# Attention and a routed expert layer on one core: first reads of scattered rows through a view of their own, weight pieces sent in another order

## The chip, the cores and the metric

One Trainium2 chip, one of its eight cores. The metric is the time of one execution on the device, in microseconds (us); each figure for the kernel is the median of several executions. The engines are PE (TensorE), with its weight loads shown as PEld, DVE (VectorE), ACT (ScalarE), POOL (GpSimd) and SP (SyncE, which here only issues DMAs). POOL issues DMAs too, the indirect ones among them. POOLq and SPq are the sequencers of these engines.

## The reference

Linear attention with a decay per head, over q, k and v of shape (4, 8, 768, 64), is computed in blocks of 64; its output, seen as 3072 tokens of 512 values, goes into a layer of 8 experts, each token to the one expert whose embedding has the largest cosine with it:

```python
for b in range(nb):
    intra = np.einsum('bhic,bhjc->bhij', qb, kb) * Dmask[None]
    out[:, :, sl] = np.einsum('bhij,bhjd->bhid', intra, vb) + np.einsum('bhid,bhde->bhie', qb * lam_pow[None], kv_state)
    kv_state = lam_block * kv_state + np.einsum('bhsd,bhse->bhde', kb * rev_pow[None], vb)
...
logits = xn @ en.T / tau                      # x and the embeddings scaled to norm 1
expert_idx = np.argmax(logits, axis=1)        # gate_w: the softmax there
out[mask] = gate_w[mask, None] * (np.maximum(x[mask] @ w1[e], 0.0) @ w2[e])
```

w1 is (8, 512, 1024), w2 (8, 1024, 512).

## The kernel before, in words

**Attention.** The 3072 tokens are 24 tiles of 128. A Python loop over rounds i = -2 to 23 writes the program out; round i finishes tile i of attention (transposes of q and k, scores, output, state) and prepares the next ones. Each engine works its own instructions strictly in the order in which they are written; semaphores between the engines are put in by the framework from what each instruction reads and writes. SP only issues loads: q, k and v into a ring of three buffers each, some rounds ahead, and staging loads. POOL scales k (`pool_ks`) and issues everything listed below.

**Routing.** The tiles are grouped (four groups of 4, four of 2). When a group's last tile is done, PE computes its logits, DVE the one-hot choice; `rt_n` (L530) takes the square root of the squared norms on POOL; PE and DVE find each token's rank within its expert (`pe_rank`, `rt_b`), DVE scales the logits by the norm (`rt_c`, L573 to L576), ACT takes the exp (L579), and DVE the gate (`rt_d`). In what follows a root is one `rt_n`. The root of the group of tiles 20 and 21 is written in round 22, the last (tiles 22 and 23) after the loop. ACT's exps stand in program order among its evictions of the first expert layer (L845).

**Scatter and read.** `scatter` (L588) writes the 128 rows of a tile by an indirect DMA into `xs_dram`, a buffer in DRAM in which each expert has its own range; a row carries the token's values in fp16, its number and its gate. Every tile scatters through its own view (`xs_views`), which the framework takes to be disjoint from the other tiles'. Reads are indirect DMAs of 128 rows (`gather`, L644) out of the whole of `xs_dram`: a read waits for all scatters written before it, and a scatter waits for all reads written before it. Experts 0 to 3 are read in two steps. `load_a` reads their first 256 rows (two reads of 128) in rounds 20 and 22, as far as the tokens of tiles 0 to 17 reach (`count("A")`); three small operations on POOL (L652, L654, L656) make the row indices ahead of each read, and rows beyond the count are skipped. `load_x` and `load_q4` read the remainder later, with indices from all tiles, and wait for the last scatter.

**Weights.** The 32 weight pieces (two per expert and matrix) come in two ways. 17 are loaded by POOL with a cast to fp16 on the way (`load_w`, L325; 8 into a weight pool, 9 into buffers of the q, k and v ring once these are done with), in a fixed order of the experts; the rounds are in the list `WP`. 15 are staged in fp32 by SP (`stage`, L338; three buffers, the first three loads in the rounds of `WS`) and cast by DVE in the tail (`cast`, `more_w`).

**Order on POOL.** A small planner (`at`, `run`) puts steps into slots of a round: `pooln` comes before `pool_ks`, `pool0` and `pool` at the round's end. In round 20 stand the reads of experts 0 and 1, in 21 the scatters of tiles 18 and 19 and three pieces, in 22 the root of tiles 20 and 21, the reads of experts 2 and 3 and three pieces, in 23 the scatters of tiles 20 and 21 and two pieces.

**The tail.** A first-step block A (256 tokens) for experts 0 to 3, then the remainders B of these, then experts 4 to 7 whole (E): transposes, first layer `pe_L1` (L842, evicted by ACT with relu, three PSUM banks), second layer `pe_L2` (L880), scaling on DVE (L860), and a scattered result on POOL (`put`, L861; five result buffers). The last 32 rows of two times four experts share blocks of their own (Q). PE starts expert 0's first layer ahead of the last group's routing. `asks` says after which block's result POOL is to issue which remaining read; a table in the function's tail writes it out.

## Time and profile before

| | us |
|---|---|
| median of 3 runs (lowest, highest) | 264.95 (262.96, 266.25) |
| the profiled execution, whole | 266.45 |
| its span, first to last instruction | 264.6 |

All rows come from the profiled execution. Times in them are us from the start of its span, if not marked ns. In a timeline a row is a run of like instructions: its start, its length, engine, line, operation, what it writes and reads, the count, and in brackets how long the engine was idle before it and what ended that. "issue" is time for which the profile shows no wait. For DMAs, the length on POOL is the time to issue them, not that of the transfer.

### The profile page before, as it was taken

The numbers are of one execution on the slowest core, as the hardware profiler recorded it, in microseconds if no ns is written. First come the engines' busy times: TensorE is split into PE (matmuls) and PEld (weight loads), VectorE is DVE, ScalarE is ACT, GpSimd is POOL, SyncE is SP. The second block draws the span as 40 slices with busy tenths as digits, with TensorE's granted clock in tenths as the row PEclk, the third lists the DMA queues.
The fourth block names the chain that finished last, engine by engine and source line by source line (L and its number), as shares of the span: only waits on it lengthen the run. The fifth ranks groups of instructions, "written<-read, shape, count | busy, mean of one in ns | idle before, by whom it ended". The sixth has DMA issues, their size and how long they took to land. (4 is left out here: it accounts for less than half of the span.)

```text
span 264.6 us, 7554 instructions
## 1 busy us (share of the span) xinstructions
PE 224.0 (85%) x3118; PEld 170.7 (65%) x3118; DVE 134.9 (51%) x367; ACT 118.6 (45%) x257; POOL 140.9 (53%) x215
## 2 busy tenths in 40 slices
PE   0889999999999999979959429987289999999990
PEld 0678888999889888857845415765067665555640
DVE  1385668579497486846604039212055539272131
ACT  5355646664755643625406022433045573644600
POOL 3375451676354648654576674278744646532332
PEclk9999999999999999999997957999869999999997
DMA  6999999999999999989339599988429996941312
GB/s 154 237 255 208 213 215 229 210 213 251 217 232 219 187 256 224 201 206 418 115 74 207 141 202 221 389 260 211 160 54 350 412 355 222 394 173 40 121 50 76
DMA packets 71684, 56.68 MB, mean 214 GB/s; under 512 B 52179, under 2 KB 64471, under 8 KB 69728
## 3 DMA queue, kind: packets, MB, share of 16 engines
q1 hardware_dynamic: 64576, 34.62, 48.6%
q0 software_dynamic: 6928, 21.55, 32.5%
q8 instruction: 25, 0.41, 0.7%
q14 instruction: 11, 0.09, 0.1%
q10 hardware_dynamic: 144, 0.00, 0.0%
HBM read 55.88 MB, written 9.99 MB: 249 GB/s over the span
## 5 line engine op out<-in xcount | busy, mean ns | idle before, releaser
L845 ACT ACTIVATE hT<-h_ps 128x416 f16<-128x416 f32 (+3 forms) x60 | 32.0, 540 | 44.3 <-PE h_ps L842 26.9
L372 POOL TENSOR_TENSOR ks<-kn,kdec 128x512 f32<-128x512 f32 x24 | 25.2, 1049 | 37.8 <-PE kaz L456 15.2
L861 POOL DMA_INDIRECT out_dram<-y_sb,tags x24 | 25.6, 1066 | 31.5 <-DVE y_sb L860 15.2
L860 DVE TENSOR_SCALAR y_sb<-y_ps,tags 128x512 f32<-128x512 f32 x24 | 18.0, 751 | 38.3 <-PE y_ps L880 28.1
L418 DVE TENSOR_TENSOR stm<-s_ps,step 128x512 f32<-128x512 f32 x48 | 30.8, 684 | 12.6 <-PE s_ps L410 12.6
L880 PEld LDWEIGHTS <-hT 128*128 128x128 f16 x192 | 18.3, 101 | 29.1 <-ACT hT L845 8.9
L842 PEld LDWEIGHTS <-w_sb 128*128 128x128 f16 x208 | 22.2, 119 | 21.5 <-issue 15.5
L880 PE MATMUL y_ps<-w_sb,hT 128*128 128x512 f16 x120 | 30.5, 404 | 6.4 <-ACT hT L845 6.1
L842 PE MATMUL h_ps<-xTe,w_sb 128*128 128x416 f16 (+2 forms) x176 | 26.2, 305 | 10.2 <-ACT hT L845 8.6
L410 PE MATMUL s_ps<-qT,kT 64*64 64x128 f32 x768 | 29.4, 284 | 1.2 <-issue 1.1
L588 POOL DMA_INDIRECT xs_dram<-xg,si x24 | 24.7, 1028 | 10.2 <-issue 4.0
L439 PE MATMUL ob<-stm,vn 128*64 128x128 f32 x384 | 26.6, 279 | 0.5 <-issue 0.5
L410 PEld LDWEIGHTS s_ps<-qT,kT 64*64 64x64 f32 x768 | 22.5, 137 | 5.7 <-issue 3.9
L439 PEld LDWEIGHTS ob<-stm,vn 128*64 128x64 f32 x384 | 20.5, 136 | 4.9 <-issue 4.7
L448 ACT COPY xT<-ob 128x256 f32<-128x256 f32 x24 | 9.0, 374 | 28.3 <-PE ob L439 27.4
L386 DVE TENSOR_TENSOR qT<-q_ps,lamq 128x512 f32<-128x512 f32 x24 | 16.4, 685 | 9.5 <-PE q_ps L384 8.1
L396 PE MATMUL k_ps<-ident,ks 128*128 128x128 f32 x96 | 15.8, 292 | 6.3 <-POOL ks L372 6.3
L644 POOL DMA_INDIRECT x<-xs_dram,rows x16 | 17.3, 1081 | 4.5 <-POOL x L662 3.0
L384 PE MATMUL q_ps<-ident,qr 128*128 128x128 f32 x96 | 17.1, 304 | 1.8 <-DVE qT L386 1.6
L398 ACT COPY kT<-k_ps 128x512 f32<-128x512 f32 x24 | 14.0, 584 | 5.5 <-PE k_ps L396 5.5
L396 PEld LDWEIGHTS k_ps<-ident,ks 128*128 128x128 f32 x96 | 12.3, 151 | 6.3 <-POOL ks L372 6.3
L481 PE MATMUL xps<-ident,xT 128*128 128x128 f32 x96 | 15.5, 277 | 1.0 <-DVE xT L449 1.0
(172 smaller groups left out, 393.8 us busy)
## 6 DMA issues: line engine op xcount, KB each, us to landing
w_st<-in_moe_w_dram SPq DMA_DIRECT2D x15, 1024.0 KB
kn<-in_k_dram SPq DMA_DIRECT2D x24, 256.0 KB
qn<-in_q_dram SPq DMA_DIRECT2D x12, 512.0 KB
vn<-in_v_dram SPq DMA_DIRECT2D x24, 256.0 KB
w_sb<-in_moe_w_dram POOLq DMA_DIRECT2D x8, 512.0 KB
kn<-in_moe_w_dram POOLq DMA_DIRECT2D x3, 512.0 KB
qn<-in_moe_w_dram POOLq DMA_DIRECT2D x3, 512.0 KB
vn<-in_moe_w_dram POOLq DMA_DIRECT2D x3, 512.0 KB
```

The costliest lines, as they stand in the source:

```text
L372: nc.gpsimd.tensor_tensor(ks[i], kn[i], kdec[:, i % RB].unsqueeze(2).to_broadcast([P, H, D]), op=ALU.mult)
L396: nc.tensor.transpose(t[:, hp, :], ks[i][:, 2 * hp : 2 * hp + 2, :].rearrange("p h d -> p (h d)"), ident)
L410: nc.tensor.matmul(bank["s", h2][ds(64 * c, 64), hp, :], kT[i][ds(64 * h2, 64), hp, ds(64 * c, 64)], q_of(i, hp)[ds(64 * h2, 64)], start=( ...
L418: nc.vector.tensor_tensor(stm[i][:, h2], bank.pop(("s", h2)), step.unsqueeze(1).to_broadcast([P, HP, P]), op=ALU.mult)
L439: nc.tensor.matmul(OB[h2][ds(64 * u, 64), b2, :], vn[i][:, 2 * hp + h2, :], stm[i][:, h2, hp, :], start=(i % RB == 0 and b2 == 0), stop=Tr ...
L588: nc.gpsimd.indirect_dma_start(out=xs_views[groups[gi][j]], out_offset=bass.IndirectOffsetOnAxis(ap=slot_i[gi][:, j : j + 1], axis=0), in_ ...
L644: nc.gpsimd.indirect_dma_start(out=out, out_offset=None, in_=xs_dram[:], in_offset=bass.IndirectOffsetOnAxis(ap=idx, axis=0), bounds_check ...
L842: nc.tensor.matmul(h_ps[:, ds(n * (fc - f0), n)], w1_cols(w, c, fc), xTe[k][:, c, 0:n], start=(fc == f0 and c == 0), stop=(c == DC - 1), s ...
L845: nc.scalar.activation(hT[k][:, f0:f1, 0:n], h_ps[:, 0 : n * (f1 - f0)].rearrange("p (f t) -> p f t", t=n), AF.Relu)
L860: nc.vector.tensor_scalar(y, y_ps, tag[:, 1:2].bitcast(FP32), None, op0=ALU.mult)
L861: nc.gpsimd.indirect_dma_start(out=out_views[n_scat[0]], out_offset=bass.IndirectOffsetOnAxis(ap=tag[:, 0:1], axis=0), in_=y[:], in_offset ...
L880: nc.tensor.matmul(y_ps, hT[k][:, fc, ds(P * (g - g_first(k)), P)], w2_rows(w, fc), start=(fc == 0), stop=(fc == FC - 1))
```

## The change

The first reads go through a view of their own, index R of one view more, so that the framework sees no overlap between them and any scatter; in its place each of these reads is made to depend by hand on the scatters of tiles 0 to 17 (`NE = 18`), recorded as they are written. `load_a` becomes one set of three index operations per expert (128x2 instead of 128x1), and `read_a` a read. POOL's order from round 20 on is written out as a list in which pieces, reads and scatters alternate: 13 pieces stand in the loop instead of 16, six of them up to round 16 and one round earlier in four cases, none in rounds 17 to 19; one follows the last root, and three instead of one stand after the last group's scatters. The three first staging loads move to round 23 of SP's order. In the tail the remaining reads are requested after other blocks.

```diff
...
     QN = P // QW
     NQ = E // QN
     GL = len(groups) - 1
-
-    WP = [3, 6, 9, 12, 14, 16, 17, 18, 21, 21, 21, 22, 22, 22, 23, 23]
-    WS = [19, 20, 20]
+    NE = 18
+    WP = [2, 5, 8, 11, 14, 16]
+    WS = [23, 23, 23]
     group_of = {}
     for gi, tl in enumerate(groups):
         for j, t in enumerate(tl):
...
     moe_t = ctx.enter_context(tc.tile_pool(name="moe_t", bufs=1))
     xs_dram = dram.tile([E * ROWS, DM2], I32, name="xs_dram")
-    xs_views = dram_disjoint_views(xs_dram[:], R)
+    xs_views = dram_disjoint_views(xs_dram[:], R + 1)
     n_out = E * GE + NQ
     out_views = dram_disjoint_views(out, n_out)
...
         nc.vector.tensor_reduce(es, rt[gi]["pe"], axis=AXL.X, op=ALU.add)
         nc.vector.reciprocal(xg[gi][:, 0:nt, DW + 1 : DW + 2].bitcast(FP32), es.unsqueeze(2))
+    written = []
     def scatter(gi, j):
-        nc.gpsimd.indirect_dma_start(
+        got = nc.gpsimd.indirect_dma_start(
             out=xs_views[groups[gi][j]],
             out_offset=bass.IndirectOffsetOnAxis(ap=slot_i[gi][:, j : j + 1], axis=0),
             in_=xg[gi][:, j, :],
             in_offset=None,
         )
+        if groups[gi][j] < NE:
+            written.append(got.ins.name)
     xe, xTe, hT = {}, {}, {}
     tags = const.tile([P, E, GE, 2], I32, name="tags")
...
                                 cnt_e.unsqueeze(2).to_broadcast([P, E, GE]), op=ALU.is_ge)
         nc.vector.scalar_tensor_tensor(rows, bad, float(OOB_IDX), row3, op0=ALU.mult, op1=ALU.add)
-    def gather(out, idx):
-        nc.gpsimd.indirect_dma_start(
-            out=out, out_offset=None, in_=xs_dram[:],
+    def gather(out, idx, src):
+        return nc.gpsimd.indirect_dma_start(
+            out=out, out_offset=None, in_=src,
             in_offset=bass.IndirectOffsetOnAxis(ap=idx, axis=0),
             bounds_check=E * ROWS - 1, oob_is_err=False)
+    after = mybir.DependencyInfo(mybir.DependencyClass.Sync, mybir.DependencyReason.DATA)
     def load_a(e):
         xe[e] = X3[e]
-        for g in range(GA):
-            nc.gpsimd.tensor_scalar(bad[:, e, g : g + 1], pos3[:, g : g + 1], cnt_a[:, e : e + 1],
-                                    float(OOB_IDX), op0=ALU.is_ge, op1=ALU.mult)
-            nc.gpsimd.tensor_tensor(bad[:, e, g : g + 1], bad[:, e, g : g + 1], row3[:, e, g : g + 1],
-                                    op=ALU.add)
-            nc.gpsimd.tensor_copy(rows_a[:, e, g : g + 1], bad[:, e, g : g + 1])
-            gather(xe[e][:, g, :], rows_a[:, e, g : g + 1])
+        nc.gpsimd.tensor_scalar(bad[:, e, 0:GA], pos3[:, 0:GA], cnt_a[:, e : e + 1],
+                                float(OOB_IDX), op0=ALU.is_ge, op1=ALU.mult)
+        nc.gpsimd.tensor_tensor(bad[:, e, 0:GA], bad[:, e, 0:GA], row3[:, e, 0:GA], op=ALU.add)
+        nc.gpsimd.tensor_copy(rows_a[:, e, :], bad[:, e, 0:GA])
+    def read_a(e, g):
+        got = gather(xe[e][:, g, :], rows_a[:, e, g : g + 1], xs_views[R])
+        for name in written:
+            tc.add_manual_dep(got.ins, name, after, reason="rows scattered so far")
     def load_x(e, g0, g1):
         if e >= ES:
             xe[e] = X3[e % ES]
             nc.gpsimd.memset(xe[e][:, g0:g1, DW : DW + 1], OOB_IDX)
         for g in range(g0, g1):
-            gather(xe[e][:, g, :], rows[:, e, g : g + 1])
+            gather(xe[e][:, g, :], rows[:, e, g : g + 1], xs_dram[:])
     def load_q4(t):
-        gather(XQ[t][:, 0, :], rowsh[:, t : t + 1])
+        gather(XQ[t][:, 0, :], rowsh[:, t : t + 1], xs_dram[:])
     def width(k):
         return {"A": CA, "B": CE - CA, "E": CE}[k[0]]
...
             at(n + 2, "z", rt_d, gi)
         else:
             at(n + 1, "end", rt_d, gi)
-    for gi, when in enumerate([(6, 7, 8, 9), (10, 11, 12, 13), (14, 15, 16, 17), (17, 18, 18, 19), (19, 19),
-                               (21, 21), (23, 23)]):
+    for gi, when in enumerate([(6, 7, 8, 9), (10, 11, 12, 13), (14, 15, 16, 17), (17, 18, 18, 19), (19, 19)]):
         for j, i in enumerate(when):
-            first = j + 1 < len(when) and when[j + 1] == i and i < 20 and gi < 4
+            first = j + 1 < len(when) and when[j + 1] == i and i < 19
             at(i, "pooln" if first else "pool", scatter, gi, j)
     for n in range(ES):
         at(1 + 2 * n, "pool", clear, X3[n])
     at(20, "pe", count, "A")
-    for i, e in ((20, 0), (20, 1), (22, 2), (22, 3)):
-        at(i, "pool0", load_a, e)
     for i in WP:
         at(i, "pool", load_w)
+    for i, fn, *a in ((20, load_a, 0), (20, read_a, 0, 0), (20, read_a, 0, 1), (20, load_w),
+                      (20, load_a, 1), (20, read_a, 1, 0), (20, load_w), (20, read_a, 1, 1),
+                      (21, scatter, 5, 0), (21, load_w), (21, scatter, 5, 1),
+                      (22, load_a, 2), (22, read_a, 2, 0), (22, load_w), (22, read_a, 2, 1), (22, load_w),
+                      (23, load_a, 3), (23, read_a, 3, 0), (23, load_w), (23, read_a, 3, 1),
+                      (23, scatter, 6, 0), (23, load_w), (23, scatter, 6, 1)):
+        at(i, "pool", fn, *a)
     for i in WS:
         at(i, "sp2", stage)
...
             nc.vector.tensor_copy(mx, nsum)
         A, B, X = [[(n, e) for e in range(E)] for n in "ABE"]
-        asks = {("A", 0, 0): [(None, 0), (0, 2), (1, 2)], ("A", 0, 1): [(2, 2), (3, 2)],
-                ("A", 1, 0): [(None, 1)]}
-        later_x = [(4, 0), (4, 1), (5, 0), (5, 1), (4, 2), (5, 2), (6, 0), (6, 1), (6, 2), (7, 0), (7, 1), (7, 2)]
-        asked_by = [("A", 2, 0), ("A", 2, 1), ("A", 3, 0), ("A", 3, 1)] + [("B", e, GA) for e in range(ES)]
-        asked_by += [("Q", 0, 0), ("E", 4, 0), ("E", 4, 1), ("E", 4, 2)]
+        asks = {("A", 1, 0): [(None, 0)], ("A", 1, 1): [(0, 2)], ("A", 2, 0): [(1, 2), (None, 1)],
+                ("A", 2, 1): [(2, 2)], ("A", 3, 0): [(3, 2)]}
+        later_x = [(4, 0), (4, 1), (4, 2), (5, 0), (5, 1), (5, 2), (6, 0), (6, 1), (6, 2), (7, 0), (7, 1), (7, 2)]
+        asked_by = [("A", 3, 1), ("A", 3, 1), ("B", 0, GA), ("B", 0, GA)] + [("B", e, GA) for e in range(1, ES)]
+        asked_by += [("Q", 0, 0), ("E", 4, 0), ("E", 4, 1), ("E", 4, 2), ("E", 5, 0)]
         for who, what in zip(asked_by, later_x):
             asks.setdefault(who, []).append(what)
...
         rt_a(GL)
         rt_a2(GL)
         rt_n(GL)
+        load_w()
         for buf in XQ:
             clear(buf)
         pe_L1(A[0], range(2, 8))
...
         pe_L2(A[0], 1)
         count("E")
         rows_of_e()
-        ask("A", 0, 0)
-        ask("A", 0, 1)
+        load_w()
+        load_w()
         load_w()
         more_w()
         more_w()
```

## Rows read from the trace of the kernel before

**Rows 1.** The page's first part: busy time, share of the span, instructions of PE.
```profile
PE 224.0 (85%) x3118; PEld 170.7 (65%) x3118; DVE 134.9 (51%) x367; ACT 118.6 (45%) x257; POOL 140.9 (53%) x215
```

**Rows 2.** The list of waits: who waited for whom, us in all, times, longest.
```profile
DVE nrm L573 <- POOL nrm L530: 16.0, 2, 10.0
...
PE h_ps L842 <- ACT hT L845: 12.4, 2, 8.6
...
ACT hT L845 <- remote: 9.0, 3, 5.1
```

**Rows 3.** PE's timeline in the seam: start, duration, work, idle time before and its releaser.
```profile
133.71 1.94 PE L842 MATMUL h_ps<-xT,w_sb 128*128 128x256 f16 x16
139.44 1.86 PE L842 MATMUL h_ps<-xT,w_sb 128*128 128x256 f16 x8 [3.79 <-ACT hT L845]
...
145.82 2.79 PE L842 MATMUL h_ps<-xTe,w_sb 128*128 128x256 f16 x24
157.24 1.86 PE L842 MATMUL h_ps<-xTe,w_sb 128*128 128x256 f16 x8 [8.62 <-ACT hT L845]
...
182.24 2.37 PE L842 MATMUL h_ps<-xTe,w_sb 128*128 128x160 f16 x32 [1.58 <-issue]
...
190.84 1.46 PE L880 MATMUL y_ps<-w_sb,hT 128*128 128x512 f16 x3 [4.87 <-ACT hT L845]
...
194.39 3.51 PE L842 MATMUL h_ps<-xTe,w_sb 128*128 128x160 f16 x32
...
199.69 2.38 PE L842 MATMUL h_ps<-xTe,kn 128*128 128x160 f16 x32
```

**Rows 4.** POOL's timeline from round 19 to the first full read.
```profile
114.39 0.96 POOL L588 DMA_INDIRECT xs_dram<-xg,si  x1 [0.31 <-issue]
...
116.87 0.19 POOL L656 CAST rows_a<-bad 128x1 int32<-128x1 f32 x1
...
121.58 1.16 POOL L644 DMA_INDIRECT x<-xs_dram,rows_a  x1 [4.52 <-DMA xs_dram<-xg,si]
...
126.86 1.10 POOL L644 DMA_INDIRECT x<-xs_dram,rows_a  x1 [0.54 <-POOL rows_a L656]
...
129.42 1.10 POOL L644 DMA_INDIRECT x<-xs_dram,rows_a  x1 [0.53 <-POOL rows_a L656]
133.23 1.03 POOL L588 DMA_INDIRECT xs_dram<-xg,si  x1 [2.71 <-DMA x<-xs_dram,rows_a]
134.57 0.99 POOL L588 DMA_INDIRECT xs_dram<-xg,si  x1 [0.30 <-issue]
135.55 1.72 POOL L325 DMA_DIRECT2D kn<-in_moe_w_dram  x3
137.26 0.78 POOL L530 TENSOR_TENSOR nrm<-nsq_all,half 128x2 f32<-128x2 f32 x1
...
151.44 1.06 POOL L588 DMA_INDIRECT xs_dram<-xg,si  x1 [1.21 <-DMA x<-xs_dram,rows_a]
...
154.99 0.76 POOL L530 TENSOR_TENSOR nrm<-nsq_all,half 128x2 f32<-128x2 f32 x1
...
170.02 1.09 POOL L644 DMA_INDIRECT xq<-xs_dram,rowsh  x1 [7.65 <-DMA xs_dram<-xg,si]
```

**Rows 5.** SP's timeline: its last v loads and the staging loads.
```profile
102.60 11.23 SPq L147 DMA_DIRECT2D vn<-in_v_dram  x3
113.87 88.33 SPq L338 DMA_DIRECT2D w_st<-in_moe_w_dram  x9
```

**Rows 6.** Stretches: busy time of each engine, granted clock (PEclk), DMA share, GB/s.
```profile
138.00:140.00 2.00, 0.56 (x3) 0.41 (x3) 1.44 (x9) 1.32 (x5) 1.09 (x5) 0.68 1.01 172
146.00:148.00 2.00, 2.00 (x20) 2.00 (x19) 0.00 (x0) 0.00 (x0) 1.27 (x4) 1.00 0.32 105
162.00:164.00 2.00, 2.00 (x10) 0.79 (x9) 2.00 (x4) 0.00 (x0) 0.36 (x1) 0.85 1.07 158
...
180.00:190.00 10.00, 4.08 (x46) 3.01 (x43) 0.75 (x1) 1.47 (x4) 7.95 (x11) 1.00 0.58 186
```

## The prediction

> **What bounds the kernel now.** I read the page first, then the waits, then the timelines of PE and POOL over the seam where attention ends and the expert layers begin. PE is busy for 85% of the span [rows 1], and outside the seam it hardly stops, so what counts is when PE gets through the seam. The list of waits names a chain: ACT's evictions of the first layer make PE wait 12.4 us in two pieces, and DVE's norms wait 16.0 us in two pieces for POOL's roots [rows 2]. The PE timeline shows the two pieces: 3.79 us ahead of 139.44 and 8.62 us ahead of 157.24 [rows 3]. Both have one cause. ACT evicts in program order behind an exp, the exp waits for DVE's scaled logits, these wait for a root on POOL, and the root stands behind everything that the rounds before put on POOL. The roots end at 137.26 + 0.78 = 138.04 and 154.99 + 0.76 = 155.75 [rows 4]; PE goes on 1.4 and 1.49 us later. So in the seam POOL's instruction order is the bound, not its arithmetic. From 194.39 PE runs at full load to the end, so what arrives earlier there ends earlier.
>
> A third stop is of another kind: ACT waits for something that the profile calls "remote", 9.0 us in three pieces [rows 2], and PE stands still for 4.87 us of it ahead of 190.84 [rows 3].
>
> **The chain on POOL, step by step.** From the first read (121.58) to the end of the last root (155.75) POOL takes 34.17 us [rows 4].
>
> Waits of scatters on reads. Scatters 18 and 20 waited 2.71 and 1.21 us for reads to land, because reads and scatters went through one view. With a view of its own for the reads, a scatter needs only the 0.30 us that the second scatter takes to be issued (133.23 + 1.03 to 134.57). Gain 2.71 + 1.21 - 0.60 = 3.32 us.
>
> Index arithmetic. Each of the eight reads has its own three small operations; from the end of one read to the start of the next that costs 1.46 us (126.86 + 1.10 to 129.42), against 0.30 us without. One set per expert remains. The first set lies ahead of the first read both times, so seven sets in the chain become three: 4 x 1.16 = 4.64 us. The operations become 128x2 instead of 128x1; at 0.2 to 0.3 us each their cost is a start-up cost, and I take no change.
>
> Weight pieces. Between the first read and the last root stood 3 + 3 + 2 = 8 issues at about 0.57 us (1.72 for three). After the change there are 7, and one more follows the root: 0.57 us. By the diff the last root's own line does not move; this piece is all it passes. No queue of SP is passed.
>
> Sum 8.53 us: the last root ends 25.6 us after the first read.
>
> The first read. It sat idle 4.52 us for scatters, the last of which was issued by 114.39 + 0.96 = 115.35. The set of rows waited for is the same as before: at round 20 only tiles 0 to 17 have been scattered. So the new dependency does not help here, but two pieces in the same queue ahead of most of those scatters, those of rounds 17 and 18, are gone. Bounds: no gain, since SP's staging loads (issued from 113.87 [rows 5]) still share the DMA engines; or 3.9 us, when the indices alone decide (116.87 + 0.19, and 0.6 to the read). A read into a quiet queue let the next scatter go 2.71 us after it. I take half, 2.0 us: first read at 119.6.
>
> The Trainium skill, DMA: Bandwidth & Descriptors, section Queues, rings and completion order, says that each DMA engine goes round-robin between queues packet by packet and works off each queue's ring in order. That speaks for the full 3.9 us here, as SP's loads then cannot stand ahead of a scatter; and against the change further down, since reads now stand behind pieces in one ring. Rows cannot separate these: the 6.2 us from 115.35 to 121.58 hold both kinds of traffic. By it the time would be 1.9 us lower, the second rival below.
>
> Last root at 119.6 + 25.6 = 145.2 instead of 155.75: 10.5 us. It lies wholly on the path, because PE waits for it both times. The earlier root (tiles 20, 21) comes 11.7 us after the first read, at 131.3, when DVE is not yet through its last attention copy; so the 3.79 us stop goes. PE then works from 133.71 without a stop: sixteen matmuls to 135.65, then what took 9.17 us (139.44 to 145.82 + 2.79), partly at half clock, in about 7.7. It stops at about 143.3 and goes on at 145.2 + 1.5 = 146.7. That wait of 3.4 us is what remains of 8.62.
>
> **What follows for PE.** Clock: after the long stop the granted clock was back at only 0.85 in 162:164 [rows 6], and the eight matmuls at 157.24 took 1.86 us where sixteen took 1.94 at 133.71 [rows 3]. From 157.24 to about 163 PE ran at 1.2 GHz, which costs 2.9 us. After the change a stop of 3.4 us stands ahead of these matmuls. The nearest row is the one at 139.44: after 3.79 us its eight took 1.86 too, but the next ones were soon at full clock again (24 in 2.79 at 145.82). Bounds 0 to 2.9 gained; I take 1.4 us.
>
> Pieces. Three pieces issued at 135.55 kept the DMA engines full (1.01 of their time at 138:140, still 0.32 at 146:148 [rows 6]): about 3 us each. Eleven pieces now leave between 121 and 153, and DVE's casts restart 3 MB of staging at about 150. Reads of expert 1 stand behind two pieces: issued by 127.4, landed by 127.4 + 6 + 2.7 = 136, and PE transposes them at about 136.6; free, by little. The second matrix of expert 3 is issued behind the last scatters and one result at about 152, and PE wants it at about 162. The last scatters before, with five pieces ahead of them, let their reader go at 170.02 only, after 7.65 us of waiting [rows 4]; so the matrix comes 0 to 5 us late. I take 2 us lost.
>
> Requests moved in the tail. POOL's 7.65 us wait ahead of 170.02 [rows 4], for the last scatters, came right behind the first expert. Now the first full read is requested one tile later and in ones and twos; POOL gets there at about 155: the root ends at 145.2, then come a piece, the clearing of two buffers, a result, two scatters, a result, three pieces and a result, some 10 us in all, the last scatter some 5 us before it. Results were queued behind that wait, but PE did not stop for them: nothing. If it waits longer, five result buffers are the cover, and beyond them DVE and PE stop.
>
> Staging loads moved to round 23. SP has nothing between its last v loads and these (11.23 us, then 113.87 [rows 5]), and their buffers are fresh, so they go out at the same time. Bounds: nothing, or the 2 us of the first read that I have not taken, if they really wait for round 23.
>
> Early pieces one round earlier. Six pieces up to round 16, both times; attention is covered by PE work, and even 2 us lost there would come out of the wait of 3.4 us, as the chain starts at scatter 17. Bounds -2 to +2, I take nothing.
>
> The third stop. From 182.24 to 194.39 expert 0's second block took 12.15 us, expert 1's 5.30 (to 199.69) [rows 3]: 6.9 us lost. No row names the cause. What stands out is POOL at 7.95 us of 10 in 180:190 [rows 6], issuing requests and results without a pause after its long wait. The new order thins this crowd. Bounds 0 and 6.9; nearest is the row that repeats under the same work, so less than half: 2.6 us.
>
> **Sum.** 10.5 + 1.4 - 2.0 + 2.6 = 12.5 us. The profiled execution took 266.45 us, of which 264.6 are span: 266.45 - 12.5 = 253.95. It was 1.5 us above the median of the runs (264.95), so I predict 252.5 us.
>
> **Rivals.**
> The third stop goes altogether (0.20): it was the crowd on POOL, and the rest holds. Another 4.3 us: 248.2.
> The first read waits for its indices alone (0.10): with no piece ahead of them the last scatters land at once. For it: the 2.71 us of the quiet queue. Against: the staging loads beside them. Another 1.9 us: 250.6.
> The reads do not come free of the scatters (0.12): the tracker still ties the new view to the whole buffer. Then the 3.32 us come back, and expert 2's reads wait some 2.7 us more for scatters 18 and 19: about 258.5. For it: the later reads still use the whole buffer. Against: scatters already use separate views and do not wait for each other.
> Pieces come later than I take them (0.14): 5 us instead of 2, and the third stop stays: 258.1.
> Slower (0.04): the one ring decides. Should each of the eleven pieces take 6 us instead of 3, beside results and staging, the last would land at 121 + 66 = 187; expert 3 waits for it, wanted at 162. The point from which this decides is 162 + 14.5 = 176.5, about 5 us per piece; at 6 it is 10.5 us over: about 275. Against: between two batches of pieces the DMA engines were at 0.32 in 146:148 [rows 6], so there is room.
>
> **How the numbers follow.** My forecast has 0.40. The low end takes the third stop (4.3), the pieces (2.0) and most of the first read (1.7) in full: 244.5. The high end takes back the first read (2.0), the third stop (2.6) and 2.4 us of pieces: 259.5. Two per cent, about what a measurement of this kernel tells from no change, is 5.3 us: faster means below 259.65. All of the forecast and of the first two rivals lie there, and most of the third and fourth: 0.88 with something off for what I do not see; within it 0.08, slower 0.04.
>
> **What would show it.** Right: no scatter waits for a read; four sets of three index operations; first read at 118 to 121.6; last root ends 25 to 26 us after it; PE's stop of 3.79 us gone and that of 8.62 under 5. A first read at 121.6 would cost 2 us. Wrong: PE waiting on weight loads at expert 3 for longer than 5 us, scatters of tiles 18 and on still waiting, or a new stop of PE in the first 120 us longer than 3.

## The result and the profile after

The changed kernel takes 253.43 us in the median of four runs (251.39 to 254.37), the kernel before 264.95 us: a ratio of 0.956, with a 95% interval of 0.946 to 0.967. Ratios, here and below, leave out executions in a second, slower state, which now and then lengthens any kernel by a few per cent. The profiled execution took 253.92 us, its span 252.1 against 264.6. So 12.5 us went between the two profiled executions, as the sum had said, but two of the four terms were far off and cancelled, and a second profile of the changed kernel (further down) shows less.

The page's first part (the row that answers to [rows 1]): PE does the same instructions in fewer busy microseconds; its mean granted clock is 0.964 instead of 0.956.

```profile
PE 220.0 (87%) x3118; PEld 167.7 (67%) x3118; DVE 136.3 (54%) x367; ACT 118.8 (47%) x257; POOL 137.5 (55%) x203
```

The list of waits (who waited for whom, us in all, times, longest). The two chains of [rows 2] have shrunk, from 16.0 to 10.4 us at the norms and from 12.4 to 6.8 at PE; ACT's wait for "remote" is gone; a wait of PE for weight pieces is new.

```profile
DVE nrm L574 <- POOL nrm L531: 10.4, 2, 7.6
PE h_ps L857 <- ACT hT L860: 6.8, 2, 6.1
PE y_ps L895 <- DMA vn<-in_moe_w_dram: 3.8, 2, 3.0
POOL x L649 <- DMA xs_dram<-xg,si: 3.5, 1, 3.5
```

POOL's timeline, to be held against [rows 4]:

```profile
116.94 0.18 POOL L662 CAST rows_a<-bad 128x2 int32<-128x2 f32 x1
120.58 1.16 POOL L649 DMA_INDIRECT x<-xs_dram,rows_a  x1 [3.46 <-DMA xs_dram<-xg,si]
125.14 1.12 POOL L649 DMA_INDIRECT x<-xs_dram,rows_a  x1 [0.55 <-POOL rows_a L662]
128.54 1.04 POOL L591 DMA_INDIRECT xs_dram<-xg,si  x1 [0.30 <-issue]
...
142.46 1.04 POOL L591 DMA_INDIRECT xs_dram<-xg,si  x1 [0.30 <-issue]
145.43 0.74 POOL L531 TENSOR_TENSOR nrm<-nsq_all,half 128x2 f32<-128x2 f32 x1
...
153.94 1.76 POOL L326 DMA_DIRECT2D vn<-in_moe_w_dram  x3
159.74 1.10 POOL L649 DMA_INDIRECT xq<-xs_dram,rowsh  x1 [2.68 <-DMA xs_dram<-xg,si]
```

No scatter waits for a read any more (0.30 us each at 128.54 and 142.46). The last root ends at 146.17, 25.59 us after the first read; before it was 34.17.

PE's timeline, to be held against [rows 3]:

```profile
133.65 1.03 PE L857 MATMUL h_ps<-xT,w_sb 128*128 128x256 f16 x8 [0.71 <-ACT hT L860]
147.57 1.87 PE L857 MATMUL h_ps<-xTe,w_sb 128*128 128x256 f16 x8 [6.08 <-ACT hT L860]
154.39 3.66 PE L857 MATMUL h_ps<-xTe,kn 128*128 128x256 f16 x32
166.31 1.04 PE L895 MATMUL y_ps<-vn,hT 128*128 128x512 f16 x4 [0.87 <-DMA vn<-in_moe_w_dram]
170.32 1.86 PE L895 MATMUL y_ps<-vn,hT 128*128 128x512 f16 x4 [2.98 <-DMA vn<-in_moe_w_dram]
173.75 0.59 PE L699 MATMUL xtr_q<-ident,xq 128*128 128x128 f16 x4 [1.56 <-DMA xq<-xs_dram,rowsh]
174.12 3.62 PE L895 MATMUL y_ps<-vn,hT 128*128 128x512 f16 x8
178.84 2.49 PE L857 MATMUL h_ps<-xTe,w_sb 128*128 128x160 f16 x32 [0.67 <-ACT xTe L716]
183.12 2.38 PE L857 MATMUL h_ps<-xTe,w_sb 128*128 128x160 f16 x32
```

From these starts and those of [rows 3] the time is balanced stage by stage:

| Stage on PE | before | after | gain | forecast |
|---|---|---|---|---|
| PE goes on behind the last root | 157.24 | 147.57 | 9.67 | 10.5 |
| from there to expert 2's first layer (clock) | 7.38 | 6.82 | 0.56 | 1.4 |
| expert 2's first layer to expert 0's second block | 17.62 | 24.45 | -6.83 | -2.0 |
| expert 0's second block | 12.15 | 4.28 | 7.87 | 2.6 |
| from there to the end of the span | 70.21 | 68.98 | 1.23 | none |

The loss in the third line is PE's waits for the pieces of expert 3's second matrix and for a half-tile read (0.87, 2.98, 1.56 us), and then eight matmuls in 3.62 us, twice the 1.89 that such a row takes at full clock (as at 167.74 in the run with spread casts below). The stretches (columns: busy time of PE, PEld, DVE, ACT and POOL, granted clock, DMA share, GB/s) say so too: the granted clock of 0.54 at 170 to 180 is close to the lower of the two levels (1.2 of 2.4 GHz).

```profile
150.00:160.00 10.00, 10.00 (x67) 6.60 (x66) 6.16 (x15) 4.37 (x7) 6.36 (x8) 0.91 0.99 305
160.00:170.00 10.00, 6.48 (x46) 4.59 (x44) 1.65 (x4) 2.39 (x4) 4.92 (x5) 0.94 1.06 282
170.00:180.00 10.00, 7.44 (x36) 3.64 (x36) 1.58 (x3) 1.48 (x4) 6.24 (x7) 0.54 0.58 202
```

From 150 to 170 the DMA engines are full. Two things are under way there: the three pieces, issued at 153.94, and the staging loads, which DVE's three casts from 150.49 on have let go on. The page's list of DMAs has the time from issue to landing (the last column, a median): the three pieces took twice as long as three of the same size before them.

```profile
150.49 0.68 DVE L349 CAST w_sb<-w_st 128x1024 f16<-128x1024 f32 x1
```

```profile
qn<-in_moe_w_dram POOLq DMA_DIRECT2D x3, 512.0 KB, 7.8
vn<-in_moe_w_dram POOLq DMA_DIRECT2D x3, 512.0 KB, 16.6
```

### The profile page after: what moved, and what is told of

Its sections match the earlier page's. It is cut to its first block, busy times and chain, and to the rows that moved or that the text cites. A ratio compares the mean times of both kernels' runs of the same rounds, so it can differ in the third digit from the quotient of the medians.

```text
span 252.1 us, 7542 instructions
## 1 busy us (share of the span) xinstructions
PE 220.0 (87%) x3118; PEld 167.7 (67%) x3118; DVE 136.3 (54%) x367; ACT 118.8 (47%) x257; POOL 137.5 (55%) x203
## 5 line engine op out<-in xcount | busy, mean ns | idle before, releaser
L857 PE MATMUL h_ps<-xTe,w_sb 128*128 128x416 f16 (+2 forms) x176 | 25.2, 296 | 6.8 <-ACT hT L860 6.1
L857 PEld LDWEIGHTS <-w_sb 128*128 128x128 f16 x208 | 20.9, 115 | 14.3 <-issue 8.4
L411 PE MATMUL s_ps<-qT,kT 64*64 64x128 f32 x768 | 28.0, 282 | 1.6 <-issue 1.5
L895 PE MATMUL y_ps<-w_sb,hT 128*128 128x512 f16 x120 | 28.5, 387 | 0.0
L411 PEld LDWEIGHTS s_ps<-qT,kT 64*64 64x64 f32 x768 | 21.5, 136 | 5.5 <-issue 3.8
```

What stands on the lines that cost most here:

```text
L411: nc.tensor.matmul(bank["s", h2][ds(64 * c, 64), hp, :], kT[i][ds(64 * h2, 64), hp, ds(64 * c, 64)], q_of(i, hp)[ds(64 * h2, 64)], start=( ...
L857: nc.tensor.matmul(h_ps[:, ds(n * (fc - f0), n)], w1_cols(w, c, fc), xTe[k][:, c, 0:n], start=(fc == f0 and c == 0), stop=(c == DC - 1), s ...
L895: nc.tensor.matmul(y_ps, hT[k][:, fc, ds(P * (g - g_first(k)), P)], w2_rows(w, fc), start=(fc == 0), stop=(fc == FC - 1))
```

## The experiments

Eleven other kernels ran and the changed one again, four at a time on one chip each, always beside the kernel before; ratios are to that. The changed kernel had 0.956 (0.946 to 0.967) at first and, on the chip of the last four, 0.965 (0.958 to 0.973).

### What the parts of the root's chain are worth

One view again, in the changed kernel:

```diff
-        got = gather(xe[e][:, g, :], rows_a[:, e, g : g + 1], xs_views[R])
-        for name in written:
-            tc.add_manual_dep(got.ins, name, after, reason="rows scattered so far")
+        gather(xe[e][:, g, :], rows_a[:, e, g : g + 1], xs_dram[:])
```

> The changed kernel, but the eight first reads go through the view of the whole buffer again, so the later scatters wait for reads to land. Theory (these waits stand on the path of the last root): scatters 18 and 20 or 19 stand still for 2 to 4 us in all, the last root ends 29 us or more after the first read instead of 25.6, and the time is 3 to 6 us above the changed kernel. Rival (PE waits later for the weight pieces of expert 3 anyway, so a later root is swallowed there): the root comes later by as much, but the time moves by less than 1 us.

Measured: 271.87 us, ratio 1.025 (1.013 to 1.036), some 6 to 7% above the changed kernel. Neither number was right: POOL's timeline shows waits of 5.30, 3.84 and 6.46 us.

```profile
134.96 1.04 POOL L591 DMA_INDIRECT xs_dram<-xg,si  x1 [5.30 <-DMA x<-xs_dram,rows_a]
143.47 1.15 POOL L649 DMA_INDIRECT x<-xs_dram,rows_a  x1 [3.84 <-DMA xs_dram<-xg,si]
158.22 1.04 POOL L591 DMA_INDIRECT xs_dram<-xg,si  x1 [6.46 <-DMA x<-xs_dram,rows_a]
161.19 0.74 POOL L531 TENSOR_TENSOR nrm<-nsq_all,half 128x2 f32<-128x2 f32 x1
```

The last root ends 39.95 us after the first read (at 121.98), 14.4 later than in the changed kernel. In the old order the reads had the ring to themselves, and a scatter waited 2.71 us for them [rows 4]; in the new one pieces stand between and ahead of the reads, and the same wait takes twice that. That the pieces are the reason is argued from the order, not tested. The theory's mechanism holds, its price doesn't.

The own view alone, in the kernel before:

```diff
-            gather(xe[e][:, g, :], rows_a[:, e, g : g + 1])
+            got = gather(xe[e][:, g, :], rows_a[:, e, g : g + 1], xs_views[R])
+            for name in written:
+                tc.add_manual_dep(got.ins, name, after, reason="rows scattered so far")
```

> The kernel before with the own view for the first reads alone; order, pieces and index operations as before. Theory: scatters 18 and 20 no longer wait (2.71 and 1.21 us), the last root ends 3.3 us earlier, 30.8 us after the first read, and the time is 3 to 4 us below the kernel before. Rival (what is gained there is given back at the weight pieces): less than 1.5 us.

Measured: 265.43 us, ratio 0.997 (0.991 to 1.002). The chain did what the theory said: from the first read at 125.47 to the end of the last root at 156.42 it is 30.95 us instead of 34.17. The time did not follow. The first read started 3.9 us later than in [rows 4], but not by its wait (4.54 us, there 4.52): in this execution the last scatter ahead of it, too, started 3.87 us later (118.26). And the third stop only moved: expert 1's second block took 11.60 us and expert 0's 5.63, together as long as before (below). Why the other executions gained nothing either is not shown. So alone the own view is worth 3.2 us of chain and hardly any time, and without it the new order loses more than it gains.

Index operations per read, in the changed kernel (one set of three 128x1 operations ahead of each read, none per expert):

```diff
-        nc.gpsimd.tensor_copy(rows_a[:, e, :], bad[:, e, 0:GA])
...
+        nc.gpsimd.tensor_copy(rows_a[:, e, g : g + 1], bad[:, e, g : g + 1])
```

> The changed kernel, but each first read has its own three index operations of 128x1 again, eight sets instead of four. Theory (seven sets against three between the first read and the last root, 1.16 us each): the last root ends 4.6 us later, 30.2 us after the first read, and the time is 4 to 5 us above the changed kernel. Rival (swallowed by the later wait for weight pieces): 0 to 1 us.

Measured: 263.11 us, ratio 0.991 (0.987 to 0.996). From the first read (121.34) to the last root's end (152.05) it takes 30.71 us, 5.12 more than in the changed kernel for four sets: 1.28 us each instead of the 1.16 of the forecast. The time rose by more than the 4 to 5 us expected. The span is 7.8 us longer; 5.9 of this is the root (the first read, too, was 0.76 later), 2.0 the stop in expert 0's second block, which takes 6.26 us here.

### Why expert 3's pieces are late

The casts spread out, in the changed kernel:

```diff
-        more_w()
-        more_w()
-        more_w()
         pe_L1(A[1])
...
+            if e == 3:
+                more_w()
             tile_of(A[e], 1)
+            if e >= 2:
+                more_w()
```

> The changed kernel, but the three casts that free the staging buffers, and with them the next 3 MB of staging loads, come after expert 2's second tile and around expert 3's instead of right behind the three pieces of expert 3's second matrix. Theory (those loads share the DMA engines with the three pieces, and so the pieces land late): the waits for pieces and for the second half-tile read at expert 3 (0.87, 2.98 and 1.56 us) and the half clock behind them go, 4 to 6 us faster than the changed kernel. Rival (the pieces are late because POOL issues them late, in one ring behind scatters and results): waits within 1 us of the same, time the same. Third: the staged weights come too late for experts 6 and 7, slower.

Measured: 251.14 us, ratio 0.950 (0.942 to 0.957); the profiled span is 247.0. On PE's timeline the waits for pieces are gone and the clock stays up (eight matmuls in 1.89 us):

```profile
152.92 3.66 PE L857 MATMUL h_ps<-xTe,kn 128*128 128x256 f16 x32
163.81 1.46 PE L895 MATMUL y_ps<-vn,hT 128*128 128x512 f16 x6
167.52 0.38 PE L699 MATMUL xtr_q<-ident,xq 128*128 128x128 f16 x4 [1.28 <-DMA xq<-xs_dram,rowsh]
167.74 1.89 PE L895 MATMUL y_ps<-vn,hT 128*128 128x512 f16 x8
170.53 2.37 PE L857 MATMUL h_ps<-xTe,w_sb 128*128 128x160 f16 x32 [0.67 <-ACT xTe L716]
```

From expert 2's first layer to expert 0's second block it is 17.61 us, as before the change (17.62), against 24.45. POOL issued the pieces at the same time (154.18). So the loss in this stage was the second batch of staging loads beside them. In the two later runs with the casts moved (below) PE does not wait for pieces either, though other stops make the stage 19.13 and 23.06 us there. By ratio the gain over the changed kernel is 0.7 to 1.6%, less than the 4 to 6 us expected, and the interval overlaps that of its first measurement; the waits in the stage settle it, not the total.

The pieces earlier, in the changed kernel:

```diff
         rt_n(GL)
         load_w()
+        load_w()
+        load_w()
+        load_w()
         for buf in XQ:
...
         rows_of_e()
-        load_w()
-        load_w()
-        load_w()
```

> The changed kernel with the three pieces of expert 3's second matrix issued at once behind the last root, ahead of the clearing of two buffers, the last two scatters and two results; some 7 us earlier. Theory (the pieces are late because they are issued late): PE no longer waits for them, 4 to 6 us faster. Rival (the one ring only changes what is late: the last scatters, the first full reads and two results now stand behind three pieces): the wait moves to the read that starts from 159.74 in the changed kernel, and the time is the same within 1.5 us or slower.

Measured: 264.49 us, ratio 0.995 (0.990 to 1.001): all of the gain is lost. PE no longer waits for pieces, but for the half-tile read, and POOL stands still for 14.02 us ahead of that read, for the last scatters (the timelines of POOL and PE):

```profile
170.56 1.09 POOL L649 DMA_INDIRECT xq<-xs_dram,rowsh  x1 [14.02 <-DMA xs_dram<-xg,si]
173.47 0.59 PE L699 MATMUL xtr_q<-ident,xq 128*128 128x128 f16 x4 [7.21 <-DMA xq<-xs_dram,rowsh]
```

The last scatters are issued by 153.84, behind the three pieces, and land by 170. In the changed kernel, ahead of the pieces, they let the reader go 2.68 us after it was there. That is the one ring of the prediction's citation (the Trainium skill, DMA: Bandwidth & Descriptors, Queues, rings and completion order: each ring is worked off in order), and here the trace agrees with it. The restarted staging loads stand beside the scatters in both kernels.

### What the third stop is

The requests, undone in the changed kernel and done alone in the kernel before; the lists of the later requests go with them, and so do two calls that ask for the first ones ahead of the last weight piece:

```diff
-        asks = {("A", 1, 0): [(None, 0)], ("A", 1, 1): [(0, 2)], ("A", 2, 0): [(1, 2), (None, 1)],
-                ("A", 2, 1): [(2, 2)], ("A", 3, 0): [(3, 2)]}
...
+        asks = {("A", 0, 0): [(None, 0), (0, 2), (1, 2)], ("A", 0, 1): [(2, 2), (3, 2)],
+                ("A", 1, 0): [(None, 1)]}
...
```

> The changed kernel with the table of requests of the kernel before: the first two full reads asked for by the first expert's first tiles, ahead of the last of the three weight pieces. Theory (the requests crowded on POOL made the stop of some 7 us in expert 0's second block): that block takes 10 us or more again and the time is 5 to 8 us above the changed kernel. Rival (the stop has another origin): the block stays near 4.3 us and the time moves by less than 1.5 us. A third reading: the last piece, behind a request that waits for the last scatters, comes some 3 us later, and PE waits 2 to 4 us more at expert 3.

> The kernel before with the table of requests of the changed kernel and nothing else. Theory (crowd of requests): expert 0's second block falls from 12.15 us to about 4.3 to 5.3, and the time is 6 to 8 us below the kernel before. Rival (the stop has another origin, or is only moved): less than 2 us.

Measured: the old requests in the changed kernel give 258.17 us, ratio 0.972 (0.962 to 0.982), with expert 0's second block at 9.00 us; the new ones in the kernel before 265.58 us, ratio 0.998 (0.993 to 1.003), with the block at 6.89 us, but stops of 2.08 and 1.16 us just ahead of it. The block moves as the theory says, the time by far less: what it gives is partly lost beside it. The requests are not the cause by themselves.

A row that all traces have tells more: POOL's wait for the last scatters, ahead of the first half-tile read (xq), and the time that experts 0 and 1 then take for their second blocks (first layer to first layer of expert 2).

| Kernel | POOL waits | two blocks take |
|---|---|---|
| changed | 2.68 | 8.44 |
| changed, pieces first | 14.02 | 17.75 |
| changed, old requests | 4.40 | 15.84 |
| before | 7.65 | 17.45 |
| before, own view | 9.78 | 17.23 |
| before, new requests | 3.41 | 11.06 |

In the other eight profiles POOL waits 0.4 to 3.0 us there, and the blocks take 8.5 to 11.4. Where POOL stands still for long, it afterwards issues reads and results without a pause, and the two blocks take longer. The wait alone does not order them: 4.40 us with the old requests goes with 15.84 us, 3.41 with 11.06. To see whether that is cause or company, eight more reads were put where PE runs at full load:

```diff
+        spare = [moe_x2.tile([P, 1, 8], FP32, name=f"spare_{n}") for n in range(8)]
...
         ask("Q", 0, 0)
+        for n in range(8):
+            gather(spare[n][:, 0, :], rows[:, n, 0:1], moe_w1.rearrange("e d (a b) -> (e d a) b", b=8))
```

> The changed kernel with eight more indirect reads on POOL (rows of 32 bytes, to buffers that nothing uses) back to back behind the first mixed result, at about 199 us, where PE runs at full load and POOL has room. Theory (while POOL issues indirect DMAs back to back, PE's signals reach ACT late, which made the third stop): between 199 and 212 PE stops for 3 us or more in all, waiting for ACT, and the time is 3 to 8 us above the changed kernel. Rival (POOL's issues do not touch PE; the stop came from something else): PE runs through and the time moves by less than 1.5 us.

Measured: 270.22 us, ratio 1.019 (1.004 to 1.033). POOL's and PE's timelines:

```profile
207.02 1.00 POOL L649 DMA_INDIRECT spare<-in_moe_w_dram,rows  x1 [0.30 <-issue]
...
216.23 1.00 POOL L649 DMA_INDIRECT spare<-in_moe_w_dram,rows  x1 [0.30 <-issue]
...
224.96 1.02 POOL L649 DMA_INDIRECT x<-xs_dram,rows  x1 [0.27 <-issue]
```

```profile
213.44 2.27 PE L858 MATMUL h_ps<-xTe,w_sb 128*128 128x416 f16 x12
221.96 1.54 PE L858 MATMUL h_ps<-xTe,w_sb 128*128 128x416 f16 x4 [6.25 <-ACT hT L861]
224.83 1.54 PE L858 MATMUL h_ps<-xTe,w_sb 128*128 128x416 f16 x4 [1.32 <-issue]
226.96 4.32 PE L858 MATMUL h_ps<-xTe,w_sb 128*128 128x416 f16 x12 [0.58 <-issue]
```

And ACT's, on which the reader looks for what released the eviction:

```profile
221.40 0.52 ACT L861 ACTIVATE hT<-h_ps 128x416 f16<-128x416 f32 x1 [9.25 <-remote]
```

PE had the first four matmuls of expert 5's first layer by about 214.2 (a third of the twelve in 2.27 us); ACT began to evict them at 221.40, 7.2 us later, and the trace knows no releaser. The layer took from 213.44 to the transposes behind it at 231.07, 17.6 us, and PE stopped for no longer than 0.58 us once POOL had issued its last (224.96 + 1.02).

The control, a POOL that is busy without DMAs in the same place:

```diff
         ask("Q", 0, 0)
+        for n in range(34):
+            nc.gpsimd.memset(XQ[0], 0)
```

> The changed kernel with 34 memsets of 0.31 us (10.5 us in all) on POOL in the place where the crowd run had eight indirect reads. Theory (it is the issuing of DMAs, not a busy POOL or its late queue, that holds up PE and ACT): PE runs through, time within 2 us of the changed kernel. Rival (a POOL queue that is 10 us late is enough): PE stops again for several us between 205 and 230, time 8 us or more above.

Measured: 272.22 us, ratio 1.015 (1.004 to 1.025), which is the rival's number, but by another wait. POOL's timeline:

```profile
211.82 15.83 POOL L1001 MEMSET xq<- 128x258 int32 x34 [4.61 <-DMA out_dram<-y_sb,xq]
```

and PE's:

```profile
213.89 5.79 PE L857 MATMUL h_ps<-xTe,w_sb 128*128 128x416 f16 x32
232.75 0.61 PE L713 MATMUL xtr<-ident,x 128*128 128x128 f16 x4 [10.89 <-DMA x<-xs_dram,rows]
```

The memsets waited 4.61 us and took 15.83, so POOL's queue was 20 us late, not 10.5, and PE at last waited for a read that stood in it. That makes the total useless as a control. The same first layer is one, though: while the memsets ran it went through in 5.79 us without a stop, ACT following at once; while DMAs were issued it took 17.6. So a busy POOL doesn't delay the hand-over between PE and ACT, and with eight more indirect DMAs on POOL it was late.

The same trace also shows that issuing back to back is not enough. Behind the memsets POOL issues nine indirect DMAs from 228.47 to 241.04 with pauses of at most 0.8 us between them, and ACT still takes up PE's work at once: PE starts the next first layer at 239.27, ACT evicts from 240.24, 0.97 us later, as it did 0.91 us after 213.89 (214.80).

```profile
240.03 1.01 POOL L876 DMA_INDIRECT out_dram<-y_sb,tags  x1 [0.30 <-issue]
```

```profile
240.24 1.16 ACT L860 ACTIVATE hT<-h_ps 128x416 f16<-128x416 f32 x2 [6.06 <-PE h_ps L857]
```

That row of DMAs is 12.6 us long; the one of the crowd run lasted from 201.01 to 225.98, 25.0 us, and the DMA engines were busier beside it (a share of 0.51 to 1.01 from 205 to 225, against 0.46 and 0.34 from 230 to 240 here). Whether the length, the traffic or something else decides, and by what path, stays open.

### Repeat, and what beats both

> The changed kernel as it is, a second time. Theory (its thinner crowd ends the third stop): expert 0's second block stays under 6 us from its first layer to expert 1's, and the pieces of expert 3 are late again by 4 to 6 us in all. Rival (the missing stop was luck of one execution): the block takes 8 us or more.

Measured: 258.70 us, ratio 0.965 (0.958 to 0.973), on a chip on which the kernel before took 268.52 in the median of the executions that it is held against. The block takes 6.70 us, between the two expectations: 1.44 and 0.52 us of stop are left. The wait for pieces is there again (2.97 and 2.07 us), and the third stage of the table above takes 25.76 us.

```profile
154.78 3.66 PE L857 MATMUL h_ps<-xTe,kn 128*128 128x256 f16 x32
...
180.54 2.37 PE L857 MATMUL h_ps<-xTe,w_sb 128*128 128x160 f16 x32 [0.67 <-ACT xTe L716]
```

Held against the same rows of the kernel before, whose profile is from another chip, the five stages give 7.23, 2.61, -8.14, 5.45 and 0.65 us here, 7.8 us of span (256.8) instead of 12.5.

On the same chip, the casts spread and SP's first staging loads behind the scatter of tile 17:

```diff
-            nc.sync.dma_start(t, w_from(spos[0]))
+            got = nc.sync.dma_start(t, w_from(spos[0]))
+            if spos[0] < NP + 3:
+                tc.add_manual_dep(got.ins, written[-1], after, reason="staging behind the scatters")
```

> The changed kernel with the three casts moved as in the run with spread casts, and in addition SP's three first staging loads wait for the scatter of tile 17, so that the scatters which the first read waits for have the DMA engines to themselves. Theory (the staging loads beside them hold the last scatters up): the first read's wait falls from 3.5 to 4.8 us to 1.5 or less, the last root ends 2 to 3 us earlier, and PE's wait ahead of it (2.28 us with spread casts) nearly goes: 1.5 to 2.5 us faster than with spread casts alone. Rival (the first read waits for the scatters' own landing): wait unchanged, 0. Second rival: the later staging now stands beside weight pieces and first reads and makes these late: slower.

Measured: 249.59 us, ratio 0.929 (0.920 to 0.937); the interval lies below the changed kernel's on this chip. From the timelines of POOL and PE, the first read and the matmuls behind the last root, first here and then in the changed kernel's second profile:

```profile
120.89 1.16 POOL L651 DMA_INDIRECT x<-xs_dram,rows_a  x1 [1.02 <-DMA xs_dram<-xg,si]
...
148.08 1.03 PE L859 MATMUL h_ps<-xTe,w_sb 128*128 128x256 f16 x8 [0.25 <-ACT hT L862]
```

```profile
122.98 1.16 POOL L649 DMA_INDIRECT x<-xs_dram,rows_a  x1 [5.38 <-DMA xs_dram<-xg,si]
...
150.01 1.03 PE L857 MATMUL h_ps<-xTe,w_sb 128*128 128x256 f16 x8 [2.68 <-ACT hT L860]
```

The wait fell from 5.38 to 1.02 us, and PE's stop ahead of the last quarter of the layer from 2.68 to 0.25: POOL's chain is hardly the bound there any more. With the casts spread alone they were 4.25 and 2.28, so it is not the casts. The staging loads beside them did hold the scatters up. What that is worth in time beyond the spread casts is not shown: those ran on another chip, with a median only 1.55 us higher (251.14) and a shorter profiled span (247.0 against 249.0).

With the later requests spread as well:

```diff
-        asked_by = [("A", 3, 1), ("A", 3, 1), ("B", 0, GA), ("B", 0, GA)] + [("B", e, GA) for e in range(1, ES)]
+        asked_by = [("B", 0, GA), ("B", 0, GA), ("B", 1, GA), ("B", 1, GA), ("B", 2, GA), ("B", 2, GA), ("B", 3, GA)]
```

> As the run with staging behind the scatters, and the reads of expert 4 and the later ones are each requested up to two tiles later, so that fewer DMAs are issued back to back on POOL around expert 0's second block. Theory (back-to-back issues on POOL make PE and ACT wait): the small stops in that block and at expert 3's (0.5, 0.3 and 1.3 us with spread casts) go, 1 to 2 us faster than without. Rival: the stops move to where the requests now are, 0 within 1 us; or the reads come late for expert 4, slower.

Measured: 253.13 us, ratio 0.940 (0.930 to 0.950), no gain. In the profiled execution, with 254.14 us one of the two longest of six, the stops are gone (expert 0's second block 4.36 us, expert 1's 4.16), but PE waited 2.10 us for a read that is now requested later, and 5.15 us ahead of the first half-tile transposes with no releaser shown. The difference to the run without is not explained, and the two intervals overlap.

## Why the prediction was right, point by point

**The chain on POOL** was right in each part. Forecast 8.53 us, measured 34.17 - 25.59 = 8.58 (25.63 from read to root in the second execution). Scatter waits: 3.22 by the run with the own view alone. Index sets: 1.28 us each against 1.16.

**The first read** came at 120.58 instead of 119.6. I had taken half of what could be gained, 2.0 us; in this execution it was a quarter (3.46 us of wait against 4.52). Even that is within the spread: the second execution waited 5.38 us, and over the eight profiles with the changed order and one index set per expert the wait is 3.46 to 5.38, against 4.52 to 4.56 in the three with the old order. So this term is not shown to be more than nothing. The bound that I named, SP's staging loads, is the cause: without them beside it the wait was 1.02 us. The rule of the Trainium skill that the prediction cites (DMA: Bandwidth & Descriptors, Queues, rings and completion order), by which each DMA engine takes turns between its queues, spoke for a first read that waits for its indices alone; the runs show that these loads hold it up all the same. The same section of the Trainium skill says, of the queues of SP and ACT, that a completion signal lands only after every earlier write of its DMA engine, across its queues, and I had not weighed it. The longer waits agree with that sentence, but no run here tells it from the plain sharing of the DMA engines.

**Staging moved to round 23** was to leave its time as it was. SP's timeline, to be held against [rows 5]:

```profile
98.32 7.35 SPq L148 DMA_DIRECT2D vn<-in_v_dram  x3
105.72 49.52 SPq L339 DMA_DIRECT2D w_st<-in_moe_w_dram  x6
```

It followed the last v loads as before, which were through 8 us sooner in this execution (the two other profiles with the old order have 106.30 and 107.03 for it); nothing waits for the round.

**The earlier root** ended at 132.25 (forecast 131.3), and 0.71 us is left of the stop of 3.79. The wait ahead of the last quarter was 6.08 us, not 3.4: attention ended some 2.7 us sooner (sixteen matmuls at 131.01, not 133.71), so PE was there early. The path did not change by that, though the prediction's own sign, a stop under 5 us, was missed here; in the second execution attention ended later and the stop was 2.68.

**Clock:** 0.56 us instead of 1.4, with a longer stop than forecast ahead. In the second execution, behind a stop of 2.68 us, the same stretch took 4.77 us, a gain of 2.61.

**Pieces: the step that failed.** "I take 2 us lost", with 0 to 5 as bounds; it was 6.83. I had looked at how full the DMA engines were between two batches and at a wait of scatters behind pieces. I had named the 3 MB of staging that restart at about 150, and put no price on them. They were the whole of it, as far as one execution shows: with the casts moved, the stage is back at 17.61 us. PE's waits on the pieces themselves, which the prediction called a sign of being wrong above 5 us, were 3.85 us in all in the first execution and 5.04 in the second.

**The third stop: the other mis-sized term.** 2.6 us were taken of 6.9; it was 7.87 in this execution and 12.15 - 6.70 = 5.45 in the second. The crowd on POOL that I named as what stands out can make such a stop, as the run with eight more reads shows; that it is the whole cause is not shown, since a shorter row of issues went by without one. I had held it for a repeating row of unknown origin. Not the requests alone thin the crowd: the last scatters now land sooner (POOL's wait 2.68 instead of 7.65 us), so less of a backlog builds up.

**The rivals.** "The third stop goes altogether" and "pieces come later than I take them" both came true, each in half of its story, and their errors, +5.3 and -4.8 us, cancelled; so did the small ones (-0.8 for the root, -0.8 for the clock, +1.2 behind the stop). That the sum came out at 12.5 us is luck in that respect, and the second execution, with 7.8 us of span and a ratio of 0.965, did not repeat it: the forecast of 252.5 us is a ratio of 0.953. "The reads do not come free of the scatters" would have been far dearer than its 258.5: the run with one view lies some 16 to 18 us above the changed kernel by the ratios. No slower end came near, though the pieces moved ahead of the last scatters show how close it lies: that one move took back the whole gain.

## What to carry to other kernels

A wait is priced in the order in which it will stand: the same scatter-behind-read wait took 2.71 us with a quiet ring and 5.30 to 6.46 us with weight pieces between the reads. When loads from two queues meet, look at what restarts the other queue (here DVE's casts), and give the urgent transfers the stretch alone, by holding the others back: the wait for the scatters fell from 4.25 to 1.02 us by that. And look at where an engine issues DMAs without a pause behind a long wait: the price may show on engines that have nothing to do with these DMAs.

## What the hardware showed unexpectedly

While POOL issued indirect DMAs back to back (1.0 us each and mostly 0.3 between) for 25.0 us, ACT began on PE's results 7.2 us late, with no releaser in the trace; a POOL busy with memsets did nothing of the kind, nor did a row of issues of 12.6 us in that run. And three staging loads of 1 MB beside them kept 128-row scatters from being seen as landed for 1 to 4 us more (waits of the first read of 2.27 to 5.38 us in twelve profiles with the loads beside them, 1.02 and 1.25 without).
